# Attention with a sparse feed-forward, head of the kernel: query blocks 0 and 1 taken together key chunk by key chunk, query weights loaded in two pieces, five VectorE tiles in these two blocks

## The chip, the core and the metric

The kernel runs on one core of a Trainium2 chip. The metric is the device time of one launch in microseconds, taken as the median of several runs. The engines are written as in the profile: PE is TensorE (matrix products), DVE is VectorE, ACT is ScalarE, POOL is GpSimd, and SP is the engine that issues most of the DMAs. Each engine works through its own list of instructions in order; semaphores connect the lists.

## What is computed

The input is one sequence of 2048 rows with 448 columns, in bfloat16. The reference is, cut to what matters:

```
xn = layernorm(x)
q  = (xn @ wq) as 16 heads of 28;   k = xn @ wk;   v = xn @ wv     # one key and value head for all
p  = softmax(q k^T / sqrt(28));     h = x + concat_heads(p v) @ wo
hn = layernorm(h);  r = hn @ w_r;   idx = the 8 rows with the largest r
y  = (silu(hn[idx] @ w_gate) * (hn[idx] @ w_up)) @ w_down * sigmoid(r[idx])
out = h + hn,  with y added to the 8 chosen rows
```

Nearly all work is in the attention: 16 heads times 2048 x 2048 exponentials.

## The kernel before

**Blocks and tiles.** The queries are cut into 16 blocks `b`: block `b` holds the 512 query rows of quarter `b // 4` for four heads (group `b % 4`). The keys are cut into 16 tiles `j` of 128 keys; four key tiles make a chunk `c`. One tile `(b, j)` needs the scores of 128 keys against 512 queries in 4 heads. They are made in two halves `p`, each by two matmuls into two banks of PSUM (`qk`).

**Two ways to the exponential.** Most tiles are taken by ACT: each half is one ACTIVATE of 128x1024 with Exp (`act_unit`, L823), into one of six buffers `P`; the two PSUM places alternate, so PE can be two halves ahead. The others are taken by DVE, which makes the exponential out of integer arithmetic (`dve_unit`, L836, and `shift`, L842): four TENSOR_SCALAR of 128x512 out of PSUM banks 4 and 5, then three shifted copies of 128x2048, 7 instructions a tile, in one of three buffers `Y`. Behind an ACT tile stand four matmuls with the values (`act_pv`), behind a DVE tile four for each of its four versions (`dve_pv`). They add up over the 16 key tiles in the bank `acc_bank(b)`, 6 or 7 by turns.

**Who takes what.** The lists `dve_tiles` and `act_tiles` are made at the end of `_main`. Block 0 has no DVE tile, most blocks have four, blocks 5, 9 and 13 have three: 57 DVE tiles and 199 ACT tiles, so 398 ACTIVATEs. Blocks are taken one after the other, key tiles in rising order.

**The head.** `chunk(c)` prepares chunk `c`: layernorm statistics of four x tiles (`bn_stats`, `bn_aggr`), the reciprocal root `rstd`, normalised rows `xn`, transposes on PE, copies `xnT`, the projection to keys with two scaled copies into `K` (one for each `p`), and the projection to values with one scaled copy into `Vs`. `chunk0` is the same for chunk 0, written out by hand in two halves `h`, with the query projection of block 0 in between and 44 matmuls on the identity ahead of it (L350, `ps<-ident`) that compute nothing that is used. Later blocks get their queries from `q_project`. The query weights come in one DMA (`wq_sb`) and are spread into the padded `wq_pad` by two copies on ACT (L405) and two on POOL (L408); every query projection reads all of `wq_pad`. After the head, `last_w` (L726 to L734) makes eight products on DVE that the last block needs.

**After a block** `post_block` copies the accumulated bank to `Ot` (L621), sends the sums through DRAM and divides; after four blocks `out_proj` makes rows of `h` and the second layernorm. The last block and the eight chosen rows have their own code at the end.

**What sets the order.** Nothing in the program's text does it directly. Every operation is recorded with an engine, a cost in nanoseconds, what it reads and writes, and a priority (`G.op`, `G.prio`). `_Graph.plan` then simulates the five engines with these costs and always starts the ready operation with the lowest priority; the lists that come out are emitted as they stand. A cost that is wrong, or a moved priority, thus changes the order on all engines, and an instruction that waits holds up all behind it on its engine. `at(t, ...)` sets the priority of an attention step by its place in the schedule, 16 units a block. Of the recorded functions, L350 is the line of every matmul, L353 that of every transpose, L364 that of every DMA from SP.

Of the kernel before, what the change touches and what calls it, by code (L numbers as in the profile page):

```python
# [6 lines left out]
ACT = mybir.ActivationFunctionType  # L7
# [223 lines left out]
def _main(nc, G, sb, ps, psb, flag, scr, xs, A_x, A_wq, A_wk, A_wv, A_wo, B_w_r, B_w_gate, B_w_up, B_w_down, out,  # L231
# [77 lines left out]
    fin = wq_sb[0:8, 0, :]  # L309
    r12 = sb("r12", [12, 128], F32)  # L310
# [56 lines left out]

    for t in range(4):
# [10 lines left out]
    G.op(PO, lambda e: e.memset(nhalf[:, :], -0.5), 100, writes=["nhalf"])  # L379
    G.op(PO, lambda e: e.iota(pidx[:, :], [[0, 1]], base=0, channel_multiplier=1), 100, writes=["pidx"])  # L380
# [4 lines left out]
    for p in range(2):  # L385
# [10 lines left out]
    G.op(AC, lambda e: e.activation(wk_rep[0:CK, :, :].rearrange("p k (i c) -> p k i c", c=32)[:, :, :, 0:DH],  # L396
                                    wk_sb[0:CK, :, :].unsqueeze(2).broadcast_to([CK, NCH, 4, DH]), ACT.Identity),
         500, reads=["wk_sb"], writes=["wk_rep"])
    G.op(AC, lambda e: e.activation(wv_pad[0:CK, :, 1:1 + DH], wv_sb[0:CK, :, :], ACT.Identity), 200,
         reads=["wv_sb"], writes=["wv_pad"])  # L400
    for ch in range(NCH):
        v = wq_pad[0:CK, ch, :, :].rearrange("p g (i c) -> p (g i) c", c=32)[:, :, 0:DH]
        w = wq_sb[0:CK, ch, :].rearrange("p (h d) -> p h d", d=DH)
        if ch % 2:
            G.op(AC, lambda e, v=v, w=w: e.activation(v, w, ACT.Identity), 480, reads=["wq_sb", "wq_pad"],  # L405
                 writes=[("wq_pad", ch)])
# [69 lines left out]
    def chunk0():  # L476
# [623 lines left out]
```

## Time and profile before

| | |
|---|---|
| median of 3 runs | 415.62 us (415.38 to 415.87) |
| profiled execution | 416.59 us, of which the span of the profile is 414.6 us |
| granted PE clock, mean | 0.967 |
| first and last ACTIVATE of the attention | starts at 15.02 us; the last stretch of 136 starts at 262.50 us and takes 126.17 us |
| ACTIVATEs with Exp of 128x1024 (L823) | 398, 368.5 us busy |
| 128x512 on DVE out of PSUM (L836) | 228, 147.2 us busy |
| shifted copies on DVE (L842) | 171, 114.7 us busy |

The span runs from the first to the last instruction; the profiled execution lies 1.99 us above its own span and 0.97 us above the median of the runs. In the profile, a row of a timeline has the start, the length, the engine, the line, the operation, the tile written and the tile read, and how many instructions of that kind follow one another; in brackets stands how long the engine had been idle ahead of it and who ended the wait. Consecutive instructions of an engine overlap a little, so the pace is the distance from one start to the next, and it is shorter than the length of one.

### The profile page before, as it was taken

The numbers are of one execution on the slowest core, as the hardware profiler recorded it, in microseconds if no ns is written. First come the engines' busy times: TensorE is split into PE (matmuls) and PEld (weight loads), VectorE is DVE, ScalarE is ACT, GpSimd is POOL, SyncE is SP. The second block draws the span as 40 slices with busy tenths as digits, with TensorE's granted clock in tenths as the row PEclk, the third lists the DMA queues.
The fourth block names the chain that finished last, engine by engine and source line by source line (L and its number), as shares of the span: only waits on it lengthen the run. The fifth ranks groups of instructions, "written<-read, shape, count | busy, mean of one in ns | idle before, by whom it ended". The sixth has DMA issues, their size and how long they took to land.

```text
span 414.6 us, 8038 instructions
## 1 busy us (share of the span) xinstructions
PE 349.3 (84%) x3295; PEld 110.5 (27%) x3295; DVE 359.5 (87%) x774; ACT 383.3 (92%) x438; POOL 49.5 (12%) x73
## 2 busy tenths in 40 slices
PE   5978798889888897889898998888888997898845
PEld 5433222222222222222222222222222221222235
DVE  5899979797978899898989999899989999999281
ACT  4779999999999999999999999999999999999640
POOL 7040001010101030100101120101010130312000
PEclk9799999999999999999999999999999999999955
DMA  7794000000000002000010002000000002001000
GB/s 206 173 235 127 2 28 2 21 8 11 20 2 27 4 25 92 27 2 29 0 29 2 7 23 92 26 3 28 2 28 0 27 4 92 28 3 27 3 30 22
DMA packets 17381, 15.73 MB, mean 38 GB/s; under 512 B 5976, under 2 KB 14460, under 8 KB 17340
## 3 DMA queue, kind: packets, MB, share of 16 engines
q1 hardware_dynamic: 17244, 15.16, 13.3%
q8 instruction: 26, 0.43, 0.5%
q14 instruction: 15, 0.12, 0.1%
q0 software_dynamic: 96, 0.02, 0.1%
HBM read 11.70 MB, written 3.47 MB: 37 GB/s over the span
## 4 chain that ended last, share of the span: by engine, by line
ACT 62%; PE 21%; DVE 12%; DMA 2%; issue 1%; SPq 1%; POOL 0%; POOLq 0%; DVEq 0%; ACTq 0%
ACT P L823 62%; PE ps L350 21%; DVE Y L836 2%; DVE Y L842 1%; DVE K L588 1%; DVE Ot L621 1%; DMA wq_sb<-in_A_wq_dram 1%; DVE xnT L581 1%; DMA Lc<-l_scr 1%; SPq L364 1%; DVE bn L547 1%; DMA l_scr<-Ot 1%; DVE xn L565 1%; DVE junk L726 1%; DVE bn L757 1%
## 5 line engine op out<-in xcount | busy, mean ns | idle before, releaser
L823 ACT ACTIVATE P<-ps 128x1024 bf16<-128x1024 f32 x398 | 368.5, 1116 | 5.1 <-PE ps L350 3.9
L350 PE MATMUL ps<-Q,K 64*128 64x512 bf16 x1024 | 182.7, 386 | 45.9 <-ACT P L823 32.3
L836 DVE TENSOR_SCALAR Y<-ps 128x512 int16<-128x512 f32 x228 | 147.2, 682 | 13.9 <-PE ps L350 13.8
L842 DVE TENSOR_SCALAR Y<-Y 128x2048 int16<-128x2048 int16 x171 | 114.7, 705 | 1.6
L350 PEld LDWEIGHTS ps<-Q,K 64*128 64x128 bf16 x1024 | 45.0, 93 | 194.9 <-ACT P L823 157.4
L350 PE MATMUL ps<-P,Vs 128*32 128x512 bf16 x796 | 79.3, 389 | 0.0
L350 PE MATMUL ps<-Y,Vs 128*32 128x512 bf16 x912 | 73.5, 381 | 0.0
L633 POOL TENSOR_TENSOR On<-Ot,Rb 128x512 bf16<-128x512 f32 x15 | 21.4, 1429 | 239.4 <-DMA Rb<-l_scr 239.4
L350 PEld LDWEIGHTS ps<-P,Vs 128*32 128x32 bf16 x796 | 20.4, 92 | 46.7 <-issue 46.6
L350 PEld LDWEIGHTS ps<-Y,Vs 128*32 128x32 bf16 x912 | 23.4, 96 | 17.6 <-issue 7.3
L350 PE MATMUL ps<-xnT,wq_pad 112*128 112x512 bf16 (+1 forms) x68 | 20.1, 393 | 0.6 <-DVE Ot L621 0.6
L350 PE MATMUL ps<-wo_pad,On 128*128 128x448 bf16 (+1 forms) x64 | 17.8, 358 | 2.3 <-DVE Ot L621 1.5
L655 POOL TENSOR_TENSOR st<-st,nhalf 128x1 f32<-128x1 f32 x12 | 10.1, 842 | 64.0 <-DVE st L653 64.0
L463 DVE TENSOR_SCALAR Q<-ps,qone 128x512 bf16<-128x512 f32 x15 | 10.9, 730 | 7.1 <-PE ps L350 7.1
L621 DVE COPY Ot<-ps 128x512 f32<-128x512 f32 x15 | 10.3, 689 | 0.9 <-PE ps L350 0.3
L649 DVE TENSOR_TENSOR hbuf<-ps,x_sb 128x448 f32<-128x448 f32 x12 | 7.5, 622 | 2.5 <-PE ps L350 2.5
L668 DVE SCALAR_TENSOR_TENSOR junk<-hbuf,st,w_rb 128x448 bf16<-128x448 f32 x12 | 8.1, 678 | 0.0
L353 PE MATMUL ps<-ident,xn 128*112 128x128 bf16 x64 | 5.3, 236 | 3.1 <-DVE xn L493 2.7
L651 DVE BATCH_NORM_STATS2 bn<-hbuf 128x6 f32<-128x448 f32 x12 | 7.5, 623 | 0.1
L350 PEld LDWEIGHTS ps<-wo_pad,On 128*128 128x128 bf16 x64 | 4.2, 97 | 11.7 <-issue 6.9
L350 PEld LDWEIGHTS ps<-xnT,wq_pad 112*128 112x128 bf16 x68 | 4.7, 104 | 9.2 <-issue 6.6
L547 DVE BATCH_NORM_STATS2 bn<-x_sb 128x6 f32<-128x448 bf16 x12 | 6.9, 605 | 0.0
(177 smaller groups left out, 169.4 us busy)
## 6 DMA issues: line engine op xcount, KB each, us to landing
Rb<-l_scr SPq DMA_DIRECT2D x15, 256.0 KB
wg_sb<-in_B_w_gate_dram SPq DMA_DIRECT2D x1, 1568.0 KB, 11.9
wu_sb<-in_B_w_up_dram SPq DMA_DIRECT2D x1, 1568.0 KB, 17.9
wd_sb<-in_B_w_down_dram SPq DMA_DIRECT2D x1, 1568.0 KB, 22.1
x_sb<-in_A_x_dram SPq DMA_DIRECT2D x3, 448.0 KB, 5.5
out_dram<-x_sb SPq DMA_DIRECT2D x3, 448.0 KB, 2.8
xn_scr<-xn SPq DMA_DIRECT2D x3, 448.0 KB, 3.8
x_sb<-in_A_x_dram SPq DMA_DIRECT2D x4, 112.0 KB, 2.1
```

Of the source, the lines that this page charges most:

```text
L350: return lambda e: e.matmul(o, lhsT=l, rhs=r, start=start, stop=stop)
L463: G.op(DV, lambda e: e.tensor_scalar(Q[:, b % 4, :], ps[:, bank, :], qone[:, 0:1], None, ALU.add), dvt(512), reads=[pk(bank), "qone"], wri ...
L547: G.op(DV, [lambda e, t=t: e.bn_stats(bn6[:, t, :], x_sb[:, t, 0:D])], 540, reads=[("x", t), ("mv", 4 * c - 1)], writes=[("bn6", t)])
L621: G.op(DV, lambda e: e.tensor_copy(Ot[:, rb, :], ps[:, acc_bank(b), :]), dvt(512), reads=[pk(acc_bank(b))], writes=[("Ot", rb)], prio=u - 30)
L633: G.op(PO, lambda e: e.tensor_tensor(On[:, qb % 2, g, :], Ot[:, rb, :], Rb[:, rb, :], ALU.mult), 1270, reads=[("Ot", rb), ("Rb", rb)], wri ...
L649: G.op(DV, lambda e: e.tensor_tensor(hbuf[:, hr, :], ps[:, bank, 0:D], x_sb[:, t, 0:D], ALU.add), dvt(D), reads=[pk(bank), ("x", t)], writ ...
L651: G.op(DV, lambda e: e.bn_stats(bn6[:, t, :], hbuf[:, hr, :]), dvt(D), reads=[("h", hr)], writes=[("bn6", t)])
L655: G.op(PO, lambda e: e.tensor_tensor(st[:, t, 4:5], st[:, t, 7:8], nhalf[:, 0:1], ALU.pow), 570, reads=[("st7", t), "nhalf"], writes=[("st ...
L668: G.op(DV, lambda e: e.scalar_tensor_tensor(junk[:, :], hbuf[:, hr, :], st[:, t, 4:5], w_rb[:, :], ALU.mult, ALU.mult, accum_out=st[:, t, ...
L823: G.op(AC, lambda e: e.activation(P[:, sl, :, :], ps[:, b0:b0 + 2, :], ACT.Exp, bias=EBIAS, scale=OCT), 905, reads=[pk(b0), pk(b0 + 1)], w ...
L836: G.op(DV, lambda e, k=k: e.tensor_scalar(Y[:, n, 0, p + 2 * k, :].bitcast(I16), ps[:, 4 + k, :], 0.0, 32639.0 - 3 * STEP, ALU.max, ALU.mi ...
L842: G.op(DV, lambda e: e.tensor_scalar(Y[:, n, v, :, :].bitcast(I16), Y[:, n, 0, :, :].bitcast(I16), v * STEP, None, ALU.add), 610, reads=[( ...
```

## The change

The change rearranges the head. All else (the tiles of blocks 2 to 15, the end) keeps its code.

- **Order of the first 32 tiles.** Instead of block 0 and then block 1, the tiles of both go chunk by chunk: four key tiles of block 0, the same four of block 1, then the next chunk. The chunks' own priorities are moved to fit (`8 * c - 3.0`, and events at `4 * c - 20`).
- **DVE tiles.** Blocks 0 and 1 have five instead of four: key tiles 5 and 9 in both blocks and 13 in block 0. That makes 58 DVE tiles and 198 ACT tiles, 396 ACTIVATEs.
- **Query weights.** They are loaded in two DMAs: the 112 columns of group 0 between the keys' and the values' weights, and the other 336 columns after them. `wq_pad` is filled group by group, group 0 on ACT, behind the second `rstd`, the three others on POOL. A query projection waits for its own group alone. `wk_rep` on ACT comes after the first `rstd`, and `wv_pad` moves from ACT to POOL.
- **Chunk 0.** All statistics come first, then the four normalised tiles; the second pair of statistics waits for the first. Order of the projections is Q, K, Q, K by halves. The scaled copies of the second half of K and the copy of the first half of Q move from ACT to DVE. 56 identity matmuls stand ahead instead of 44, and 16 more (`warm(4)` four times) between the transposes.
- **Chunk 1** gets `rstd` from POOL (`pow`) like chunks 2 and 3, no longer from two ACT instructions. Chunks 1 to 3 use two PSUM banks (4 and 5) by turns, no longer three, and their key projection is recorded in two pieces.
- **Query projections** of blocks 1, 2 and 3 get places of their own: that of block 1 in bank 4, that of block 2 in bank 4 at 24.0, that of block 3 at 34.5. `last_w` has the priority of 72 instead of 40.

The list that the planner makes of this can be read from the built program: on PE, 58 identity matmuls stand ahead of the first transpose and 2, 7, 1 and 4 behind the four groups of transposes; the first score matmuls of a DVE tile stand behind those of the 30th ACTIVATE (before: behind the 21st), and on DVE all DVE tiles stand behind the value copy of chunk 3, as before.

```diff
     for t in range(4):
-        dma(x_sb[:, t, 0:D], x_v[:, t, :], [("x", t)], lat=2700.0 + 250 * t)
-    dma(wk_sb[0:CK, :, :], A_wk.rearrange("(k p) n -> p k n", p=CK), ["wk_sb"], lat=4000.0)
-    dma(wv_sb[0:CK, :, :], A_wv.rearrange("(k p) n -> p k n", p=CK), ["wv_sb"], lat=4000.0)
-    dma(wq_sb[0:CK, :, :], A_wq.rearrange("(k p) n -> p k n", p=CK), ["wq_sb"], lat=5500.0)
+        dma(x_sb[:, t, 0:D], x_v[:, t, :], [("x", t)], lat=2700.0 + 350 * t)
+    dma(wk_sb[0:CK, :, :], A_wk.rearrange("(k p) n -> p k n", p=CK), ["wk_sb"], lat=4500.0)
+    dma(wq_sb[0:CK, :, 0:CK], wq_v[:, :, 0:CK], [("wq", 0)], lat=5000.0)
+    dma(wv_sb[0:CK, :, :], A_wv.rearrange("(k p) n -> p k n", p=CK), ["wv_sb"], lat=5500.0)
+    dma(wq_sb[0:CK, :, CK:D], wq_v[:, :, CK:D], [("wq", 1)], lat=6500.0)
...
+    for _ in range(56):
+        G.op(PE, mm(ps[:, 7, 0:128], ident[:, :], ident[:, :], True, True), 85, reads=["ident"], writes=[pk(7)])
...
-    for ch in range(NCH):
-        v = wq_pad[0:CK, ch, :, :].rearrange("p g (i c) -> p (g i) c", c=32)[:, :, 0:DH]
...
+    def pad_wq(g, eng):
+        v = wq_pad[0:CK, :, g, :].rearrange("p k (i c) -> p k i c", c=32)[:, :, :, 0:DH]
+        w = wq_sb[0:CK, :, g * CK:g * CK + CK].rearrange("p k (i d) -> p k i d", d=DH)
...
-        for _ in range(44):
-            G.op(PE, mm(ps[:, 7, 0:128], ident[:, :], ident[:, :], True, True), 107, reads=["ident"], writes=[pk(7)],
-                 prio=-900)
...
+        q_half(0)
+        k_half(0, AC)
+        q_half(1)
+        k_half(1, DV)
         v_project(0, 5)
-        G.prio = 9
-        q_project(1, MISC)
+        G.prio = -0.5
+        q_project(1, 4)
...
-        G.prio = 4 * c - 7
+        G.prio = 8 * c - 3.0
...
-            return (7, 4, 5)[hb[0] % 3]
+            return 4 + hb[0] % 2
...
-    groups[0] = 0
+    FD, FN, FT, FS = (5, 9, 13), 5, 18.5, 2.8
...
+    first = [(b, j) for c in range(4) for b in range(2) for j in range(4 * c, 4 * c + 4)]
+    early = [(b, j) for j in FD for b in range(2)][:FN]
+    for n, (b, j) in enumerate(early):
+        dve_tiles.append((b, j, FT + FS * n))
+    left = [p for p in first if p not in early]
+    for n, (b, j) in enumerate(left):
+        act_tiles.append((b, j, 32.0 * n / len(left)))
+    for b in range(2, NB):
...
-    events = [(4.0 * c - 9.0, lambda c=c: chunk(c)) for c in range(4)]
+    events = [(4.0 * c - 20.0, lambda c=c: chunk(c)) for c in range(4)]
...
-        if b + 2 < NB:
+        if 1 < b < NB - 2:
             at(16 * b + 6.5, q_project, b + 2, misc_bank(b))
...
-    at(16 * 2 + 8.0, last_w)
+    at(24.0, q_project, 2, 4)
+    at(16 * 2 + 2.5, q_project, 3, misc_bank(2))
+    at(16 * 4 + 8.0, last_w)
```

More of the change, by code (lines that the diff above doesn't have):

```diff
@@ L474, in v_project, with warm @@
                                            ALU.mult), 620, reads=[pk(bank), "vcc"], writes=[("V", c)])
+    def warm(n, prio):
+        for _ in range(n):
+            G.op(PE, mm(ps[:, 7, 0:128], ident[:, :], ident[:, :], True, True), 80, reads=["ident"], writes=[pk(7)],
+                 prio=prio)
     def chunk0():
         G.prio = -500
[L478 to L480 removed]
@@ new lines, in q_half @@
+            bank = 6 + h
+            G.op(PE, [mm(ps[:, bank, 0:256], wq_pad[0:CK, ch, 0, :], xnT[0:CK, 0, ch, c], ch == 0, ch == NCH - 1)
+                      for ch in range(NCH)], 4 * 115, reads=[("wqp", 0), ("xnT", 0, 2 * h), ("xnT", 0, 2 * h + 1)],
+                 writes=[pk(bank)])
+            G.op(DV, lambda e: e.tensor_scalar(Q[:, 0, c], ps[:, bank, 0:256], qone[:, 0:1], None, ALU.add), 400,
+                 reads=[pk(bank), "qone"], writes=[(("Q", "Qh")[h], 0)])
+        q_half(0)
```

136 lines of the change are left out of this document (65 added, 71 removed).

## The prediction

> **What bounds the kernel now.** I read the page first: shares of the engines, the chain that ended last, the costliest groups.
>
> ```profile
> span 414.6 us, 8038 instructions
> ...
> PE 349.3 (84%) x3295; PEld 110.5 (27%) x3295; DVE 359.5 (87%) x774; ACT 383.3 (92%) x438; POOL 49.5 (12%) x73
> ...
> ACT 62%; PE 21%; DVE 12%; DMA 2%; issue 1%; SPq 1%; POOL 0%; POOLq 0%; DVEq 0%; ACTq 0%
> ...
> L823 ACT ACTIVATE P<-ps 128x1024 bf16<-128x1024 f32 x398 | 368.5, 1116 | 5.1 <-PE ps L350 3.9
> L836 DVE TENSOR_SCALAR Y<-ps 128x512 int16<-128x512 f32 x228 | 147.2, 682 | 13.9 <-PE ps L350 13.8
> L842 DVE TENSOR_SCALAR Y<-Y 128x2048 int16<-128x2048 int16 x171 | 114.7, 705 | 1.6
> ```
>
> ACT leads, DVE is near. An average hides the stages, so next come the windows view of the exponentials alone (L823), and that of all engines over the attention.
>
> ```profile
> 15.00:39.74 24.74, 21.11 (x22) 0.99 0.84 199
> 39.74:388.70 348.96, 347.35 (x376) 1.00 0.07 22
> ```
>
> ```profile
> 40.00:388.00 348.00, 303.30 (x2749) 82.54 (x2745) 313.59 (x617) 346.43 (x376) 34.39 (x29) 1.00 0.07 22
> ```
>
> From 39.74 us on ACT is full: 376 exponentials in 347.35 us, a **pace of 0.924 us** each, with 1.6 us of gaps. The first 22 took 24.74 us where the pace gives 20.3: **4.4 us are lost in the head**, and the first one starts only at 15.02. DVE is idle 348.0 - 313.6 = **34.4 us** of the body. So the body is bound by the number of ACT exponentials; the head is bound by what feeds them. ACT's timeline and the chain that ended last, over the head, tell by what:
>
> ```profile
> 6.38 0.20 ACT L489 ACTIVATE rstd<-var 128x2 f32<-128x2 f32 x1
> 7.74 1.04 ACT L405 ACTIVATE wq_pad<-wq_sb 112x448 bf16<-112x448 bf16 x2 [1.06 <-DMA wq_sb<-in_A_wq_dram]
> 8.78 1.06 ACT L501 ACTIVATE xnT<-ps 112x512 bf16<-112x512 bf16 x2
> 14.11 1.02 ACT L525 ACTIVATE K<-ps,kb,ksc 128x256 bf16<-128x256 f32 x2 [1.18 <-PE ps L350]
> 15.02 1.94 ACT L823 ACTIVATE P<-ps 128x1024 bf16<-128x1024 f32 x2
> 20.51 2.87 ACT L823 ACTIVATE P<-ps 128x1024 bf16<-128x1024 f32 x3 [0.53 <-PE ps L350]
> 25.14 4.93 ACT L823 ACTIVATE P<-ps 128x1024 bf16<-128x1024 f32 x5 [1.76 <-PE ps L350]
> 39.75 222.25 ACT L823 ACTIVATE P<-ps 128x1024 bf16<-128x1024 f32 x240 [0.34 <-PE ps L350]
> ```
>
> ```profile
> 3.60 4.06 DMA wq_sb<-in_A_wq_dram
> ...
> 10.66 3.43 PE ps L350 x16
> ...
> 23.94 1.43 DVE K L588 x2
> ...
> 30.30 1.44 DVE K L588 x2
> ...
> 35.98 1.46 DVE K L588 x2
> ```
>
> The chain runs: the one DMA of the query weights (landed at 7.66), the pads on ACT, which hold up the second `rstd` and the first `xnT`, then 16 projection matmuls in 3.43 us, then the first exponential. After that the chain goes through DVE: the keys of chunks 1, 2 and 3 are there at 25.4, 31.7 and 37.4, and block 0 alone eats a chunk in 8 exponentials, 7.4 us. ACT waits for DVE's chunks, through PE.
>
> **Part 1, the start of the exponentials.** The DMA and the pads leave the chain: group 0 has a quarter of the bytes, and its one pad stands behind both `rstd`. What is late next is PE's list, where 58 identity matmuls come first.
>
> ```profile
> 1.80 4.28 PE L350 MATMUL ps<-ident 128*128 128x128 bf16 x44 [1.80 <-POOL ident L377]
> 20.08 0.61 PE L350 MATMUL ps<-Q,K 64*128 64x512 bf16 x4
> ```
>
> ```profile
> 5.00:6.00 1.00, 1.00 (x16) 0.90 (x14) 0.41 (x3) 0.62 (x2) 1.00 (x12) 1.00 0.66 143
> 7.00:8.00 1.00, 0.74 (x8) 0.58 (x8) 0.32 (x2) 0.26 (x1) 0.29 (x1) 1.00 1.12 308
> 12.00:13.00 1.00, 1.00 (x6) 0.70 (x5) 0.18 (x1) 0.93 (x3) 0.00 (x0) 0.50 0.34 88
> 5.30:8.70 3.40, 1.51 (x21) 1.18 (x19) 0.81 (x3) 2.22 (x8) 1.69 (x11) 1.00 1.01 301
> 387.60:391.00 3.40, 2.81 (x19) 0.94 (x17) 0.76 (x2) 1.19 (x3) 0.00 (x0) 1.00 0.00 0
> 391.00:394.40 3.40, 1.82 (x6) 0.68 (x6) 2.38 (x10) 1.90 (x6) 0.00 (x0) 1.00 0.03 5
> ```
>
> The 44 end at 6.08; 14 more at the pace of the last ones (16 in 1 us, 0.0625) take 0.9, at the mean pace (4.28 / 44 = 0.097) 1.4: they end between 6.95 and 7.45; I take 6.95, since the last ones are the nearest. The first `rstd` was done at 6.58 behind two pads that now stand elsewhere, so `xn` is no later than that. Eight transposes took 0.74, so the first tile's are through at 7.35 and the second's, behind 2 more identity matmuls, at 7.8. ACT: `xnT` 0.53 (1.06 / 2), pad 0.52 (1.04 / 2), `xnT` 0.53: 7.4 to 9.0. Meanwhile transposes three and four, with 8 identity matmuls between, end near 8.9, and DVE's two copies near 9.5:
>
> ```profile
> 2.83 1.15 DVE L482 BATCH_NORM_STATS2 bn<-x_sb 128x6 f32<-128x448 bf16 x2 [1.01 <-DMA x_sb<-in_A_x_dram]
> 10.27 0.85 DVE L504 COPY xnT<-ps 112x512 bf16<-112x512 bf16 x2 [0.47 <-PE ps L353]
> 13.26 0.48 DVE L520 TENSOR_SCALAR Q<-ps,qone 128x256 bf16<-128x256 f32 x1 [1.08 <-PE ps L350]
> 60.08 1.28 DVE L836 TENSOR_SCALAR Y<-ps 128x512 int16<-128x512 f32 x2
> 61.27 1.28 DVE L842 TENSOR_SCALAR Y<-Y 128x2048 int16<-128x2048 int16 x2
> 62.48 0.69 DVE L836 TENSOR_SCALAR Y<-ps 128x512 int16<-128x512 f32 x1
> ```
>
> The 16 projections ran at a granted clock of 0.50 (12 to 13 us). At full clock they take half of 3.43: from 9.05 to about 10.8. Behind them on DVE stand one copy of Q (0.48), one `bn_stats` (1.15 / 2) and the other copy of Q: the second half of Q is there near 11.0. The last two K copies no longer stand ahead of the exponential on ACT. From score matmuls to the exponential are 0.43 (20.08 to 20.51): first exponential at **11.6**; at half clock at 9.05 + 3.43 + 0.5 + 0.43 = 13.4. Which clock? It had fallen after a stretch of 3.4 us in which PE was busy 1.51 (5.30 to 8.70), and fell again after one with 1.82 (391.0 to 394.4), while one with 2.81 (387.6 to 391.0) left it at 1.00. After the change PE has work all through 5.3 to 8.9. So it should hold: 11.6, **3.4 us earlier**.
>
> [...]
>
> **Part 2, gaps in the head.** Chunks are now needed at exponentials 17, 29 and 41 (8 tiles, then 6, then 6 on ACT), that is at 11.6 + 16 x 0.924 = 26.4, then 37.5 and 48.6. DVE had the keys at 25.4, 31.7 and 37.4; its copies of `xnT`, from which its chain goes on, end near 9.5 instead of at 11.1, and it gets two K copies of 0.51 and a Q copy of 0.48 more to do, and ahead of the keys of chunk 3 three products of `last_w` that stood behind them, 0.60 each if they are like Y. So the keys come at about 25.3, 31.6 and 39.1, and no chunk is late, the first by a margin of 1.1. What remains is order on PE: some score matmuls stand behind transposes of the next chunk. I keep 0.5 of the 4.4 us: **-3.9**. Bounds: 0 and 2.3 (the two largest gaps, 0.53 and 1.76, come back).
>
> **Part 3, one tile less on ACT:** 2 exponentials, **-1.85**. The seven instructions more on DVE take 0.60 each (60.08, 61.27, 62.48: two and two in 2.40), 4.2 us, beside 34.4 us of idle time.
>
> **Part 4, DVE loses its lead.**
>
> ```profile
> 38.53 1.29 DVE L836 TENSOR_SCALAR Y<-ps 128x512 int16<-128x512 f32 x2
> ```
>
> ```profile
> PEld ps L350 <- DVE Y L836: 15.6, 37, 1.2
> DVE Y L836 <- PE ps L350: 13.8, 25, 1.1
> ```
>
> Its tiles start where they did, at 38.5, but there ACT stood at exponential 22, and now at 30. Until the list has caught up, PE, which keeps order, holds score matmuls for ACT behind matmuls on DVE's results. By the order of the built program the worst place is exponential 65, behind the values of the third shifted copy of tile (2, 1). For that copy DVE has 44 instructions of 0.60 (26.4), two copies to `Ot` and two of Q at about 0.66 (2.6), small ones (0.4), and waits for PE of 13.8 / 25 = 0.55 at some six score pairs (3.3 to 3.6): done at 38.5 + 32.9 = 71.4, and three groups of value matmuls later the scores can run: 72.5. ACT would be there at 11.6 + 0.5 + 64 x 0.924 = 71.2. That and a smaller one before give **+1.7**. After it a block has 28 x 0.60 + 1.7 = 18.5 us on DVE against 24 x 0.924 = 22.2 on ACT, and DVE gains again. Bounds: 0 (exponentials start later and DVE is in time) and 4.3 (0.06 more for each of the 44, as the groups' means of 147.2 / 228 = 0.646 and 114.7 / 171 = 0.671 have it).
>
> **Edits costed at nothing.** POOL's pads, `wv_pad` and `rstd` of chunk 1 lie beside 88% idle on POOL; a late `rstd` would delay chunk 1, with its margin of 1.1. The added DMA moves the x loads on SP by one issue (0.43 to 0.49):
>
> ```profile
> 4.00:5.00 1.00, 1.00 (x13) 1.00 (x11) 0.00 (x0) 1.00 0.78 58
> ```
>
> Here the narrow `wk` and `wv` rows kept the DMA engines busy 0.78 at 58 GB/s; the later x tiles are first read behind the first copy of Q, near 10. If they land 1 us late, that stands ahead of the second copy of Q and costs 1 us. [...]
>
> **Sum:** -3.4 - 3.9 - 1.85 + 1.7 = -7.45. Span 414.6 to 407.15; the execution is 1.99 longer than its span (416.59), so 409.1; the median of the runs is 0.97 below the profiled one, so **408.2 us**.
>
> **Rivals.**
> - *The start comes at half clock* (0.13). PE's busy time is modelled and the bound lies somewhere between 1.82 and 2.81 of 3.4; then 13.4 instead of 11.6: **410.0**. For it: a single stretch decides. The same would follow if the clock rose later than in the row from 5 to 6 us, since the identity matmuls then end later and the projections run slow. Against: the three runs lie within 0.5 us. [...]
> - *DVE's catching up costs 4.3* (0.15): **410.8**, and 412.5 if block 3 pays as well. For it: PE's weight loads already wait 15.6 us for Y. Against: ACT hardly noticed.
> - *DVE sets the end* (0.06), the slower side. If DVE from 38.5 on had no idle time, its one tile more would add 7 x 0.60 = 4.2: **419.8**. It decides once the 34.4 us of idle time are used up by waits; nothing in the trace takes that much.
> - *The gains are swallowed by PE's order in the head* (0.04): Part 2 and Part 4 at their worst and the half clock together, 415.6 - 1.6 - 2.1 - 1.85 + 4.3 = **414.4**, or no change if one more place of 1.2 comes.
>
> **Chances and range.** Forecast 0.62, with its own range of 406.4 to 409.6. A run of this kernel tells 0.2% from no change. Faster 0.91, same 0.03, slower 0.06. The range takes in the first two rivals above and, below, Part 4 at 0 with a start at 11.1: **405.5 to 412.5**.
>
> **What would show it.** Right: a first exponential between 11.2 and 12; granted clock 1.00 from 9 to 12; the 23rd exponential near 32.4 instead of 39.75; ACT's largest gap near 70 us, behind PE; 396 ACTIVATEs. Wrong: `xnT` waiting for identity matmuls; DVE's first statistics of chunk 1 waiting for a DMA; gaps of ACT after 100 us, behind Y; an ACT pace above 0.93.

## The result, and the profile after

The changed kernel takes **412.36 us** (median of 6 runs, 411.80 to 414.31) where the kernel before took 415.75 beside it (6 runs, 415.07 to 416.82): a ratio of 0.9928, 95% interval 0.9906 to 0.9949. That is 3.4 us faster. The forecast was 408.2, with an own range of 406.4 to 409.6; the sign was right, the gain was under half of the one forecast, and the wider range of 405.5 to 412.5 just holds the measured time. A second measurement (`e7_after_again`, below) gave 412.64 us, ratio 0.9944 (0.9920 to 0.9968).

The profiled execution took 414.31 us, the longest of the six; its span is 412.2. The page, with the shares of the engines, the chain that ended last, and the costliest groups:

```profile
span 412.2 us, 8124 instructions
...
PE 352.7 (86%) x3335; PEld 110.9 (27%) x3335; DVE 366.0 (89%) x785; ACT 381.1 (92%) x429; POOL 51.3 (12%) x76
...
ACT 54%; PE 27%; DVE 16%; issue 1%; DMA 1%; POOL 0%; SPq 0%; POOLq 0%; DVEq 0%
...
L845 ACT ACTIVATE P<-ps 128x1024 bf16<-128x1024 f32 x396 | 368.1, 1089 | 6.3 <-PE ps L351 4.3
...
L858 DVE TENSOR_SCALAR Y<-ps 128x512 int16<-128x512 f32 x232 | 149.5, 680 | 13.2 <-PE ps L351 12.7
L864 DVE TENSOR_SCALAR Y<-Y 128x2048 int16<-128x2048 int16 x174 | 119.0, 715 | 1.5
```

The lines have moved by some twenty: L845 is now the exponential, L858 the DVE copy out of PSUM, L864 the shifted copy, L351 the matmuls. Two exponentials less, as announced, yet ACT's share of the last chain went from 62 to 54% and PE's from 21 to 27%: ACT waits for PE more often (ahead of exponentials 8 times, 4.3 us in all, where it was 6 times and 3.9 us). ACT's timeline tells where:

```profile
10.86 1.02 ACT L527 ACTIVATE K<-ps,kb,ksc 128x256 bf16<-128x256 f32 x2 [1.14 <-PE ps L351]
12.40 53.81 ACT L845 ACTIVATE P<-ps 128x1024 bf16<-128x1024 f32 x58 [0.52 <-PE ps L351]
66.48 1.94 ACT L845 ACTIVATE P<-ps 128x1024 bf16<-128x1024 f32 x2 [0.27 <-PE ps L351]
69.25 1.94 ACT L845 ACTIVATE P<-ps 128x1024 bf16<-128x1024 f32 x2 [0.83 <-PE ps L351]
72.23 56.40 ACT L845 ACTIVATE P<-ps 128x1024 bf16<-128x1024 f32 x61 [1.04 <-PE ps L351]
```

The head is as forecast: one run of 58 exponentials without a gap, 53.81 / 58 = 0.928 us each; the five gaps of before between 20 and 40 us are gone. New are the gaps at 66 to 72 us. The windows view of the exponentials alone, for the same 22 us in the kernel after and, below it, before (columns: length, busy time with the number of instructions, granted clock, DMA share, GB/s):

```profile
55.00:77.00 22.00, 19.74 (x22) 1.00 0.06 16
```

```profile
55.00:77.00 22.00, 22.00 (x25) 1.00 0.05 14
```

To add up such losses over a whole execution I take the starts of the exponentials from the trace and subtract 0.9167 us from each step; 24 steps in 22.0 us is what the undisturbed blocks of before need. What is left over in a stretch is its loss. Steps are counted from the first exponential. "Last" is the end of the last exponential. All numbers are us, each row is one profiled execution; steps 25-48 lose nothing in any of them (0.4 in `e1`). From the fourth row on they are the experiments that follow.

| kernel | exps | first | steps 1-24 | 49-72 | 73-216 | from 217 | last |
|---|---|---|---|---|---|---|---|
| before | 398 | 15.02 | 4.55 | 0.01 | 1.08 | 3.20 | 388.67 |
| after, first profile | 396 | 12.40 | 0.12 | 2.82 | 4.14 | 3.69 | 386.22 |
| after, second profile (`e7_after_again`) | 396 | 11.63 | 0.12 | 2.83 | 2.81 | 3.89 | 384.32 |
| `e1_four_tiles` | 398 | 11.09 | 0.31 | 1.61 | 3.02 | 3.17 | 384.52 |
| `e2_not_merged` | 398 | 12.46 | 6.76 | 0.41 | 1.58 | 3.21 | 389.23 |
| `e3_fewer_identity` | 396 | 11.06 | 3.98 | 2.82 | 2.81 | 2.60 | 386.32 |
| `e4_block2_three` | 398 | 11.89 | 0.13 | 2.14 | 1.17 | 3.77 | 383.98 |
| `e5_short_shifts` | 396 | 11.52 | 0.12 | 2.82 | 3.29 | 3.78 | 384.57 |
| `e8_block2_lc` | 398 | 12.55 | 2.56 | 2.03 | 2.43 | 2.99 | 387.43 |
| `e9_tile_9` | 396 | 11.70 | 0.13 | 2.28 | 1.26 | 7.03 | 385.44 |
| `e11_short_told` | 396 | 11.63 | 0.13 | 2.27 | 1.53 | 2.99 | 381.60 |
| `e13_eight_p` | 396 | 11.99 | 0.13 | 1.20 | 2.12 | 4.18 | 382.68 |
| `e16_eight_p_lc` | 396 | 11.41 | 0.12 | 1.31 | 3.41 | 3.51 | 382.81 |
| `e17_eight_p_three` | 398 | 11.38 | 0.13 | 0.65 | 1.12 | 3.31 | 381.47 |
| `e15_before_eight_p` | 398 | 12.92 | 4.46 | 0.00 | 2.78 | 2.52 | 387.47 |
| `e18_before_warm` | 398 | 12.99 | 4.46 | 0.00 | 1.70 | 2.44 | 386.38 |

The first profile of after has 1.3 us of its 4.14 from a half clock at 157.7 to 161.1 us, which the second does not have; so the second is the one to compare with. It is, however, the fastest of its twelve runs.

### The profile page after: what moved, and what is told of

Read it like the earlier page. It is cut to its first block, busy times and chain, and to the rows that moved or that the text cites. A ratio compares the mean times of both kernels' runs of the same rounds, so it can differ in the third digit from the quotient of the medians.

```text
span 412.2 us, 8124 instructions
## 1 busy us (share of the span) xinstructions
PE 352.7 (86%) x3335; PEld 110.9 (27%) x3335; DVE 366.0 (89%) x785; ACT 381.1 (92%) x429; POOL 51.3 (12%) x76
## 3 DMA queue, kind: packets, MB, share of 16 engines
HBM read 11.70 MB, written 3.47 MB: 37 GB/s over the span
## 4 chain that ended last, share of the span: by engine, by line
ACT 54%; PE 27%; DVE 16%; issue 1%; DMA 1%; POOL 0%; SPq 0%; POOLq 0%; DVEq 0%
ACT P L845 53%; PE ps L351 27%; DVE Y L858 7%; DVE Y L864 6%; DVE Ot L636 1%; DMA Lc<-l_scr 1%; DVE bn L772 1%; ACT K L527 0%; DVE idx L972 0%; ACT xn L789 0%; POOL out_dram L1038 0%; DVE On L630 0%; SPq L365 0%; DVE wq_sb L1037 0%; DVE ra L778 0%
## 5 line engine op out<-in xcount | busy, mean ns | idle before, releaser
L845 ACT ACTIVATE P<-ps 128x1024 bf16<-128x1024 f32 x396 | 368.1, 1089 | 6.3 <-PE ps L351 4.3
L351 PE MATMUL ps<-Q,K 64*128 64x512 bf16 x1024 | 183.0, 386 | 42.1 <-ACT P L845 29.5
L858 DVE TENSOR_SCALAR Y<-ps 128x512 int16<-128x512 f32 x232 | 149.5, 680 | 13.2 <-PE ps L351 12.7
L864 DVE TENSOR_SCALAR Y<-Y 128x2048 int16<-128x2048 int16 x174 | 119.0, 715 | 1.5
L351 PEld LDWEIGHTS ps<-Q,K 64*128 64x128 bf16 x1024 | 43.9, 93 | 188.2 <-ACT P L845 146.8
L351 PE MATMUL ps<-P,Vs 128*32 128x512 bf16 x792 | 78.4, 390 | 0.0
L351 PE MATMUL ps<-Y,Vs 128*32 128x512 bf16 x928 | 77.7, 382 | 0.1
L648 POOL TENSOR_TENSOR On<-Ot,Rb 128x512 bf16<-128x512 f32 x15 | 22.4, 1496 | 235.9 <-DMA Rb<-l_scr 235.9
L351 PEld LDWEIGHTS ps<-P,Vs 128*32 128x32 bf16 x792 | 20.1, 93 | 46.1 <-issue 45.5
L351 PEld LDWEIGHTS ps<-Y,Vs 128*32 128x32 bf16 x928 | 23.6, 95 | 24.5 <-issue 12.4
L351 PE MATMUL ps<-xnT,wq_pad 112*128 112x512 bf16 (+1 forms) x68 | 19.3, 377 | 1.4 <-DVE Ot L636 1.2
L351 PE MATMUL ps<-wo_pad,On 128*128 128x448 bf16 (+1 forms) x64 | 17.8, 358 | 2.6 <-DVE Ot L636 1.8
L351 PE MATMUL ps<-ident 128*128 128x128 bf16 x72 | 7.6, 287 | 1.8 <-POOL ident L380 1.8
L351 PEld LDWEIGHTS ps<-ident 128*128 128x128 bf16 x72 | 6.9, 134 | 1.8 <-POOL ident L380 1.8
L351 PEld LDWEIGHTS ps<-wo_pad,On 128*128 128x128 bf16 x64 | 4.2, 97 | 11.8 <-issue 7.9
L351 PEld LDWEIGHTS ps<-xnT,wq_pad 112*128 112x128 bf16 x68 | 4.4, 98 | 10.2 <-issue 4.2
```

Of the source, the lines that this page charges most:

```text
L351: return lambda e: e.matmul(o, lhsT=l, rhs=r, start=start, stop=stop)
L648: G.op(PO, lambda e: e.tensor_tensor(On[:, qb % 2, g, :], Ot[:, rb, :], Rb[:, rb, :], ALU.mult), 1270, reads=[("Ot", rb), ("Rb", rb)], wri ...
L845: G.op(AC, lambda e: e.activation(P[:, sl, :, :], ps[:, b0:b0 + 2, :], ACT.Exp, bias=EBIAS, scale=OCT), 905, reads=[pk(b0), pk(b0 + 1)], w ...
L858: G.op(DV, lambda e, k=k: e.tensor_scalar(Y[:, n, 0, p + 2 * k, :].bitcast(I16), ps[:, 4 + k, :], 0.0, 32639.0 - 3 * STEP, ALU.max, ALU.mi ...
L864: G.op(DV, lambda e: e.tensor_scalar(Y[:, n, v, :, :].bitcast(I16), Y[:, n, 0, :, :].bitcast(I16), v * STEP, None, ALU.add), 610, reads=[( ...
```

## The experiments

**First round: is it VectorE's lag, or the clock?** Theory A: DVE has lost its lead, and PE, which keeps order, holds ACT's scores up behind it. Theory B: the loss comes from the late rise of PE's clock at the start (7.51 us) and a dip later (0.50 from 157.7 to 161.1 us), both seen in the first profile. Four kernels take the change apart. Before, measured beside them: 415.42 us.

`e1_four_tiles`: no fifth DVE tile.

```diff
-    FD, FN, FT, FS = (5, 9, 13), 5, 18.5, 2.8
+    FD, FN, FT, FS = (5, 9, 13), 4, 18.5, 2.8
```

> The changed kernel with four instead of five DVE tiles in blocks 0 and 1 (key tiles 5 and 9 of both); ACT has 398 exponentials again, 1.85 us more than the changed kernel (412.4). Theory A, DVE lost its lead and holds ACT's score matmuls up through PE's order: the gaps at 57 to 75 us (2.8 us beyond the pace) mostly go and the body after 100 us loses 1 to 2 us less, so 410 to 412.5. Theory B, the shortfall is the PE clock (a late rise at the start, a dip in the body) and DVE's load does not matter: 414.2, with the gaps at 57 to 75 us as they were.

Measured: 413.07 us, ratio 0.9932 (0.9911 to 0.9954). The fifth tile brings at most part of its 1.85: what two exponentials more cost here, the stretch 49-72 gives back in good part (2.8 to 1.6). That decides nothing between A and B, but gaps remain with one DVE tile less.

`e2_not_merged`: all parts of the change but the merging (and its DVE tiles).

```diff
-    first = [(b, j) for c in range(4) for b in range(2) for j in range(4 * c, 4 * c + 4)]
-    early = [(b, j) for j in FD for b in range(2)][:FN]
+    first = []
+    early = []
...
-    for b in range(2, NB):
+    groups[0] = 0
+    for b in range(NB):
```

> The changed kernel with blocks 0 and 1 one after the other and their tiles shared out as before (none on DVE in block 0, four in block 1); 398 exponentials; all else of the change stays. If taking the two blocks together is what feeds ACT in the head: first exponential still near 12.4, but 3 to 4.4 us of gaps from there to 40 us, as before, and few gaps at 57 to 75 us: 414 to 416. If the start alone made the gain (rival): the gaps merely moved, and 412 to 413.5.

Measured: 416.53 us, ratio 1.0021 (0.9995 to 1.0048). Nothing of the gain is left, although the first exponential is at 12.46. ACT's timeline shows who took it back:

```profile
12.46 7.52 ACT L846 ACTIVATE P<-ps 128x1024 bf16<-128x1024 f32 x8 [0.52 <-PE ps L351]
23.88 1.94 ACT L846 ACTIVATE P<-ps 128x1024 bf16<-128x1024 f32 x2 [3.90 <-PE ps L351]
26.31 2.17 ACT L846 ACTIVATE P<-ps 128x1024 bf16<-128x1024 f32 x2 [0.49 <-PE ps L351]
```

Block 0 alone has eaten chunk 0 after 8 exponentials, at 20.0, and chunk 1 comes when it comes: 3.90 us of waiting. Here the earlier start is worth nothing, since nothing is there to do until the next chunk. The two gains of the head are not two independent terms: without the merging, the first is lost. (The 6.76 us of this profile are not owed to the missing merging alone: the granted clock was 0.50 from 24.7 to 31.5 us, behind the longest gap. And `e18` below shows that a head in which the chunks come earlier too keeps an earlier start.)

`e3_fewer_identity`: 44 identity matmuls ahead instead of 56, none between the transposes.

```diff
-    for _ in range(56):
+    for _ in range(44):
...
-            warm(4, -500)
+            warm(0, -500)
```

> The changed kernel with 44 identity matmuls ahead, as before, and none between the transposes. If these matmuls only stand in the way of the transposes: the first transpose starts near 6.5 instead of 7.7 and the first exponential near 11.3 instead of 12.4, and the time is 411 to 412. If they keep the clock up (rival): the granted clock is 0.50 during the 16 projections, the first exponential is at 12.8 to 13.5 and the time 412.5 to 414.

Measured: 412.26 us, ratio 0.9913 (0.9882 to 0.9945), no difference from after. Its profiled execution did start early, at 11.06, and lost it again at 21 us, in a way that no theory had. DVE's timeline, then the windows of all engines (columns: PE, PEld, DVE, ACT, POOL busy, granted clock, DMA share, GB/s):

```profile
20.87 0.62 DVE L451 TENSOR_REDUCE sw<-w_rb 128x1 f32<-128x448 bf16 x1 [1.95 <-DMA w_rb<-in_B_w_r_dram]
```

```profile
18.30:21.60 3.30, 1.68 (x18) 0.81 (x16) 1.35 (x4) 3.03 (x4) 0.00 (x0) 1.00 0.97 271
21.70:28.40 6.70, 6.26 (x42) 1.55 (x42) 5.92 (x17) 3.60 (x4) 2.42 (x3) 0.50 1.04 235
```

A sum over the router's weights, needed at the end of the kernel, stands in the middle of DVE's head and waited 1.95 us for its DMA; behind it stood the last copy of `xnT` for chunk 1, PE ran dry (1.68 of 3.30 busy), and the clock went to 0.50 for 6.8 us. That is one execution, the slowest of its four runs (411.98 to 414.05); the median does not show it.

`e4_block2_three`: three DVE tiles in block 2 instead of four.

```diff
+    groups[2] = 3
     where = {0: (), 1: (9,), 2: (5, 11), 3: (3, 7, 11), 4: (1, 5, 9, 13), 5: (1, 4, 7, 10, 13)}
```

> The changed kernel with three instead of four DVE tiles in block 2 (five stay in blocks 0 and 1); 398 exponentials. Theory A (lead): DVE catches up one tile, 4.2 us, sooner, the gaps at 57 to 66 us stay (0.9 us), those at 66 to 75 us go, and the body loses 1 to 2 us less: 410.5 to 412.5. Theory B (clock): 414.2.

Measured: 411.92 us, ratio 0.9902 (0.9868 to 0.9936). Two exponentials more cost 1.83 us, and the kernel is no slower: the loss in steps 73-216 fell from 2.8 to 1.17, about what before has (1.08). So one DVE tile in block 2 is worth nothing, and the losses after step 72 hang on it. That is what A said of this stretch; whether DVE is late on the chip or the planner writes another order is left to `e5` and `e11`. In steps 49-72 2.14 of 2.83 remain, and that is not what A said.

**Second round: take VectorE's work away.** If A also holds for the gaps at 57 to 75 us, they must shrink when DVE has less to do there. Before, measured beside these: 415.55 us.

`e5_short_shifts`: the shifted copies of eight DVE tiles leave out three quarters of their columns; the planner is told nothing of it, so all lists keep their order.

```diff
-        G.op(DV, lambda e: e.tensor_scalar(Y[:, n, v, :, :].bitcast(I16), Y[:, n, 0, :, :].bitcast(I16),
+        w = 1 if 3 <= m < 11 else 4
+        G.op(DV, lambda e: e.tensor_scalar(Y[:, n, v, 0:w, :].bitcast(I16), Y[:, n, 0, 0:w, :].bitcast(I16),
```

> The changed kernel with the shifted copies of eight VectorE tiles (numbers 3 to 10) cut to a quarter of their columns, the order of all instructions unchanged; what is left out is three quarters of these copies, about 24 x 0.45 = 10.8 us of VectorE's time between 52 and 130 us. Theory A (VectorE falls behind in the merged blocks and through PE's order holds ScalarE's scores up): the gaps of 2.8 us at 57 to 75 us shrink to 1 or less and the excess of the steps from 72 to 216 from 1.7 to about 1: 408.0 to 409.5. Theory B (the order on PE or the clock makes these gaps by itself): they stay, 411.5 to 412.5.

Measured: 412.35 us, ratio 0.9932 (0.9906 to 0.9958): nothing gained, in steps 73-216 either (3.29 us lost, 2.81 in `e7`), of which the short copies cover the part up to some 130 us. **Theory A falls for these gaps.** The 24 copies did get short (the groups view, shapes apart), and ACT's gaps came at the same exponentials with the same lengths to 0.01 us:

```profile
L865 DVE TENSOR_SCALAR Y<-Y 128x512 int16<-128x512 int16 x24 | 6.1, 285 | 0.1
```

```profile
66.58 0.68 DVE L636 COPY Ot<-ps 128x512 f32<-128x512 f32 x1
67.91 0.40 PE L351 MATMUL ps<-P,Vs 128*32 128x512 bf16 x4
68.36 1.94 ACT L845 ACTIVATE P<-ps 128x1024 bf16<-128x1024 f32 x2 [0.83 <-PE ps L351]
71.34 1.94 ACT L845 ACTIVATE P<-ps 128x1024 bf16<-128x1024 f32 x2 [1.04 <-PE ps L351]
```

`e7_after_again`: the changed kernel, unaltered.

> The changed kernel as it is, for a second profile on the same chip as the others: 411.8 to 413. If the time of the clock's rise sets the start, a run that rises before 5.5 us has its first exponential at 11.0 to 11.3, and one that rises after 7 us near 12.4; the gaps at 57 to 75 us are the same 2.8 us either way.

Measured: 412.64 us, ratio 0.9944 (0.9920 to 0.9968); the profiled execution took 411.84. The first exponential came between the two expected places, at 11.63, and the gaps are the same 2.8 us. The whole timeline around the largest gaps, cut to the instructions that matter:

```profile
65.82 0.62 PE L351 MATMUL ps<-Y,Vs 128*32 128x512 bf16 x8
...
67.10 0.68 DVE L636 COPY Ot<-ps 128x512 f32<-128x512 f32 x1
...
67.70 0.10 PEld L351 LDWEIGHTS ps<-Q,K 64*128 64x128 bf16 x2 [0.37 <-ACT P L845]
...
68.02 0.40 PE L351 MATMUL ps<-P,Vs 128*32 128x512 bf16 x4
...
68.47 1.94 ACT L845 ACTIVATE P<-ps 128x1024 bf16<-128x1024 f32 x2 [0.83 <-PE ps L351]
...
71.01 0.39 PE L351 MATMUL ps<-P,Vs 128*32 128x512 bf16 x4
...
71.45 1.94 ACT L845 ACTIVATE P<-ps 128x1024 bf16<-128x1024 f32 x2 [1.04 <-PE ps L351]
```

Read it backwards from 68.47, with the code beside it. This is the 61st exponential. Its scores had been made at 66.8, so it does not wait for scores. It writes buffer 60 % 6 = 0 of the six `P`, which the 55th wrote for key tile (2, 0); the value matmuls of that tile, at 68.02 to 68.42, must have read it. The built program says the same: its 61st and 63rd exponential wait for the value matmuls of block 2 that read P buffers 0 and 2. Of the 2.83 us, these two steps hold 0.93 and 1.14; of the rest, 0.49 before the 51st is a wait for a P buffer too, which value matmuls of block 0 have to read, and 0.39 before the 59th is a wait for scores. The value matmuls of block 2 are that late because they open the accumulator of block 2, `acc_bank(2)` = bank 6, which is that of block 0 as well. Block 0 ends only with the last version of its DVE tile (0, 13), at 65.82 to 66.44, and DVE copies the bank to `Ot` at 67.10. In the kernel before, block 0 was long done by then (the copies to `Ot` start at 50.00 for block 0 and 71.86 for block 1); merged, blocks 0 and 1 hold both banks until the end (62.90 and 67.10).

**Theory C**: ACT fills its six buffers, three key tiles, and then waits for the first value matmuls of block 2; and these stand where the written order has them, behind score matmuls that themselves wait for ACT (67.70). This explains `e5`: the copy to `Ot` came 0.4 us sooner there, counted from the first exponential, and the value matmuls stayed where the list has them. The accumulator thus acts through the written order: the planner puts these matmuls behind the copy in its own simulation.

**Theory D**: PE simply has too much work there. The windows view has it full for 4 us, though not for the next two:

```profile
62.00:64.00 2.00, 2.00 (x24) 0.50 (x22) 1.97 (x4) 2.00 (x3) 0.00 (x0) 1.00 0.00 0
64.00:66.00 2.00, 2.00 (x16) 0.62 (x14) 2.00 (x5) 1.73 (x3) 0.00 (x0) 1.00 0.01 4
66.00:68.00 2.00, 1.52 (x14) 0.39 (x10) 2.00 (x4) 1.65 (x2) 0.00 (x0) 1.00 0.04 4
```

`e8_block2_lc`: as `e4`, and the planner is told longer times for the two DMAs of a block's sums.

```diff
-            dma(scr[b, 0], Ot[0:128:32, rb, :], [("scr0", b)], reads=[("Ot", rb)])
-        dma(Lc[:, rb, :], scr[b, 0].rearrange("i (r k) -> (i r) k", k=16), [("Lc", rb)], reads=[("scr0", b)])
+            dma(scr[b, 0], Ot[0:128:32, rb, :], [("scr0", b)], reads=[("Ot", rb)], lat=3000.0)
+        dma(Lc[:, rb, :], scr[b, 0].rearrange("i (r k) -> (i r) k", k=16), [("Lc", rb)], reads=[("scr0", b)], lat=3500.0)
```

> Block 2 with three VectorE tiles, and the planner told that the two DMAs of a block's sums take 3.0 and 3.5 us instead of 2.0 each, so that VectorE meets the minimum, maximum and reciprocal of the sums later. Theory A: VectorE's waits for these DMAs of up to 1.9 us, behind which Y and then the scores stand, go away and the single long steps with them: 410.5 to 411.3. Rival: they are hidden nearly always, 411.9 as with three tiles in block 2 alone.

Measured: 412.17 us, ratio 0.9919 (0.9887 to 0.9950), as `e4` within the interval, and not the 410.5 to 411.3 of A. (Its profiled execution, 415.25, is the slowest of its eight and had 7 us of half clock in the head, which its steps 1-24 show.)

`e9_tile_9`: a DVE tile moved from block 2 to block 9.

```diff
+    groups[2], groups[9] = 3, 4
```

> One VectorE tile moved from block 2 to block 9: 396 exponentials as in the changed kernel, but VectorE gets 4.2 us back in the catch-up and pays them at 240 us. Theory A (only the lead is short in the catch-up): the gaps at 56 to 80 us as with three tiles in block 2 (2.1), the excess to 216 us near 1, 410 to 411. Rival (VectorE has no idle time to spend in any block): a gap of over 1 us near block 9 and 411.5 to 412.5.

Measured: 412.78 us, ratio 0.9921 (0.9892 to 0.9951), 0.3 above the rival's range and far from that of A. Steps 73-216 are as cheap as in `e4` (1.26), and from 217 on 7.03 us are lost where after has 3.89; ACT waits 1.04 us at the ninth exponential of block 10, which follows the full block:

```profile
254.37 56.82 ACT L846 ACTIVATE P<-ps 128x1024 bf16<-128x1024 f32 x61 [1.04 <-PE ps L351]
```

One half-clock stretch of 3.4 us at 340 us is in these 7.03 too. Neither of the two blocks tried, 2 and 9, takes the fourth tile for nothing.

**Third round: the buffers.** Before, beside these: 415.54 us.

`e13_eight_p`: eight buffers `P` instead of six. (The room comes from `idi`, a helper of the start that now lies in a buffer used later.)

```diff
-    NPB = 6
+    NPB = 8
...
-    idi = sb("idi", [128, 128], I32)
...
     hbuf = sb("hbuf", [128, 4, D], F32)
+    idi = hbuf[:, 0, 0:128].bitcast(I32)
```

> The changed kernel with eight P buffers instead of six, so that ScalarE can be four key tiles ahead of the value matmuls and not three. Theory C: ScalarE's gaps before exponentials 61 and 63 (0.9 and 1.1 us), which end with value matmuls of block 2, go, the gaps at 57 to 75 us fall from 2.8 to 1 or less: 410.0 to 411.0. Theory D (PE is full there) or A (VectorE late): the gaps come elsewhere, 412 to 412.5.

Measured: **410.11 us**, ratio 0.9865 (0.9840 to 0.9891). That is faster than both kernels (the kernel after had ratios of 0.9928 and 0.9944). The exponentials in the same 22 us as above, and ACT's timeline:

```profile
55.00:77.00 22.00, 21.30 (x24) 1.00 0.06 16
```

```profile
11.99 59.41 ACT L845 ACTIVATE P<-ps 128x1024 bf16<-128x1024 f32 x64 [0.52 <-PE ps L351]
72.00 19.52 ACT L845 ACTIVATE P<-ps 128x1024 bf16<-128x1024 f32 x21 [0.61 <-PE ps L351]
```

ACT is busy 21.30 of 22.00 us where it was 19.74, and the stretch 49-72 loses 1.20 instead of 2.83, a little more than the 1 that C allowed. D said that the gaps come elsewhere; most do not. The edit also moves PE's list, since the planner knows of the eight buffers. But block 0 is copied no sooner, counted from the first exponential, and the value matmuls of key tile (2, 0) come even later than in `e7` (68.02), while ACT runs on:

```profile
67.54 0.69 DVE L636 COPY Ot<-ps 128x512 f32<-128x512 f32 x1
...
68.86 0.40 PE L351 MATMUL ps<-P,Vs 128*32 128x512 bf16 x4
```

The largest gap left, 0.61 at 72.00, stands before the 65th exponential; in the built program that one waits for a P buffer again.

`e15_before_eight_p`: the same edit in the kernel before.

> The kernel before with eight P buffers. Theory C: its blocks end one after the other, its accumulator comes free in time and no exponential waits for a P buffer, so nothing is gained: 415.0 to 416.0. If eight buffers help every block (more slack on PE), it gains 1 to 3 us as well and the gain of eight buffers in the changed kernel is not owed to the merging.

Measured: 415.69 us, ratio 1.0011 (0.9990 to 1.0032). Eight buffers are worth nothing there, and the lists of the built program are those of before, entry by entry. So of these two kernels the six bind only in the one that merges two blocks: **C stands**, for the gaps before the 61st and the 63rd exponential.

`e11_short_told`: the short copies of `e5`, and the planner knows that they are short.

```diff
-                                           v * STEP, None, ALU.add), 610,
+                                           v * STEP, None, ALU.add), 610 if w > 1 else 270,
```

> The same shortened shifted copies as before (eight VectorE tiles, three quarters of each copy left out), and now the planner is told that such a copy takes 0.27 us instead of 0.61, so that PE's written order may use VectorE's time. The shortening alone left the gaps of ScalarE at 57 to 75 us as they were, since the order was already written. Theory C (a block's accumulator and six P buffers: block 2's first value matmuls must wait until block 0's last ones are through and copied, ScalarE fills six P buffers meanwhile and then waits): block 0 ends some 2 us earlier, the gaps fall from 2.8 to about 1.5 and the time to 410.5 to 411.5. Theory D (PE simply has too much work there): 412 to 412.5.

Measured: 410.11 us, ratio 0.9869 (0.9843 to 0.9895), 2.2 us less than `e5` with the same instructions in another order. The time is a little better than C had it, but not for C's reason: the gain lies mostly in the stretches behind. 73-216 fell from 3.29 to 1.53, 49-72 only from 2.82 to 2.27, where C had about 1.5; the copy of block 0 came 1.2 us sooner than in `e7` (65.89 for 67.10), not 2. So DVE's time does count, but through the order that the planner writes with it; shorter copies in the old order gained nothing.

`e16_eight_p_lc`: eight buffers and the longer DMA times of `e8`.

> The changed kernel with eight P buffers and with the planner told that the two DMAs of a block's sums take 3.0 and 3.5 us. If both help, 409.5 to 410.5; if the waits for these DMAs are hidden, as eight P buffers alone.

Measured: 410.54 us, ratio 0.9877 (0.9852 to 0.9902), as eight buffers alone within the interval. The profiles speak against the longer times, both here and in `e8`: steps 73-216 lose 1.3 us more with them (3.41 for 2.12, and 2.43 for 1.17).

**Fourth round: what was still open.** Before, beside these: 415.81 us.

`e17_eight_p_three`: eight buffers and three DVE tiles in block 2.

> The changed kernel with eight P buffers and with three VectorE tiles in block 2: both remedies. If the lost time between exponentials 72 and 216 (2.1 us with eight P buffers) comes from block 2's fourth VectorE tile, it falls to about 1.1, while two exponentials more cost 1.83: 410.0 to 411.0, the two remedies do not add up. If they do: 409.0 to 409.7.

Measured: 410.80 us, ratio 0.9879 (0.9844 to 0.9914), the first of the two cases: the losses fall to 0.65 and 1.12, the lowest of all, and two exponentials more take that back. It does not beat `e13`.

`e18_before_warm`: the kernel before, with 20 identity matmuls in PE's idle time between the transposes.

```diff
+                for _ in range(20 if t == 1 else 0):
+                    G.op(PE, mm(ps[:, 7, 0:128], ident[:, :], ident[:, :], True, True), 2, reads=["ident", ("xn", t)], writes=[pk(7)])
```

> The kernel before with 20 identity matmuls more, between the first two pairs of transposes, where PE was idle for 1.75 us; nothing else is changed and no other order moves. If the half clock in the head is what most of the executions of before pay, the granted clock stays 1.00 from 5 to 14 us, the first exponential comes at 12.9 to 13.3 instead of 15.0, and the time is 413.5 to 414.5: then some 1 to 2 us of the forecast's 3.4 at the start belong to the clock alone. If it is an accident of the one profiled execution: 415.2 to 415.8.

Measured: 414.49 us, ratio 0.9969 (0.9948 to 0.9989). The windows from 9 to 12 us, before and then with the 20 matmuls:

```profile
9.00:12.00 3.00, 2.45 (x16) 2.02 (x17) 2.53 (x6) 1.30 (x3) 1.44 (x10) 0.50 0.66 208
```

```profile
9.00:12.00 3.00, 2.44 (x24) 2.03 (x24) 2.78 (x7) 2.09 (x5) 1.45 (x10) 1.00 0.73 237
```

PE is as busy in both, but at full clock it does 24 matmuls instead of 16, and the first exponential comes at 12.99 instead of 15.02. So 2.0 of the 3.4 us at the start are the clock's alone, in this pair of executions; in the medians the 20 matmuls are worth 1.3 (0.5 to 2.2 by the interval). The whole head moves with the clock: the 9th exponential, the first that needs chunk 1, starts at 23.02 instead of 25.14.

## Why the prediction was right in sign and too high in size

Its sum, beside what the two profiles (before 416.59; the second profile of after, 411.84, the fastest of its runs) show:

| step | forecast | measured |
|---|---|---|
| start of the exponentials | -3.4 | -3.4 (15.02 to 11.63; first profile 12.40, -2.6) |
| gaps in the head | -3.9 | -4.4 |
| one tile less on ACT | -1.85 | -1.83 |
| catching up, steps 49-72 | +1.7 | +2.8 |
| steps 73-216 | 0 | +1.7 |
| steps from 217, and the end | 0 | +0.7 - 0.4 |
| sum | -7.45 | -4.7 |
| from the profiled pair to the medians | -0.97 | none; the median of after lies 0.5 to 0.8 above its second profile |

- **Right:** the full clock from 9 to 12 us (1.00 in the first profile), the 23rd exponential (32.4 forecast; 32.72 and 31.95), 396 ACTIVATEs, the head without gaps, the largest gap of ACT near 70 us behind PE. The first exponential (11.6 forecast, a band of 11.2 to 12) came at 12.40 and 11.63; the near hit is luck in part, since the place of the clock's rise, taken from one execution, moves it (4.56 us in `e1`, with the first exponential at 11.09, and 7.51 in the first profile of after, with 12.40).
- **Wrong, the step that after the catch-up a block has 18.5 us on DVE against 22.2 on ACT, "and DVE gains again".** The sums of the windows view over 13 blocks, 78 to 372 us after and 80 to 372 before:

```profile
sum 294.00, PE 257.37 PEld 68.65 DVE 275.53 ACT 290.63 POOL 31.48; mean PE 19.80 PEld 5.28 DVE 21.19 ACT 22.36 POOL 2.42
```

```profile
sum 292.00, PE 255.57 PEld 69.42 DVE 267.93 ACT 290.50 POOL 28.98; mean PE 19.66 PEld 5.34 DVE 20.61 ACT 22.35 POOL 2.23
```

  DVE has 21.2 us of work in a stretch of 22.6 (294 / 13), about one block, not 18.5 in 22.2. The row for it stood in the profile before: DVE 20.6. The 18.5 counted the tiles, `Ot` and Q, and left out the rows of the output that four blocks later go through DVE:

```profile
L664 DVE TENSOR_TENSOR hbuf<-ps,x_sb 128x448 f32<-128x448 f32 x12 | 7.4, 616 | 0.6 <-PE ps L351 0.6
L666 DVE BATCH_NORM_STATS2 bn<-hbuf 128x6 f32<-128x448 f32 x12 | 7.4, 620 | 0.1
L677 DVE TENSOR_SCALAR x_sb<-hbuf,st 128x448 bf16<-128x448 f32 x12 | 6.1, 508 | 0.0
L680 DVE TENSOR_SCALAR xn<-hbuf,st 128x448 bf16<-128x448 f32 x12 | 6.1, 506 | 0.0
L683 DVE SCALAR_TENSOR_TENSOR junk<-hbuf,st,w_rb 128x448 bf16<-128x448 f32 x12 | 8.1, 677 | 0.0
```

  35.1 us over 12 blocks, 2.9 each. With 1.4 us of slack, waits included, DVE can hardly regain its lead, and the loss goes on until step 216: +1.7. The runs show that this loss goes with the order that the planner writes from DVE's costs: `e4` and `e11` take it away, `e5`, shorter copies in the old order, does not. That the small slack is what makes this order is argued, not shown. The planner's own simulation of the two programs, with its 0.905 us an exponential, already has both losses: 0.13 us before and 3.51 after in steps 49-72, 2.34 and 3.82 in steps 73-216. The +0.7 behind step 216 is not explained; the other kernels without a dip there lose 2.4 to 4.2.
- **Wrong mechanism, the step that a shifted copy is done at 71.4 "and three groups of value matmuls later the scores can run".** The place was near, the cause another: not scores behind a late DVE copy (`e5`), but, for 2.07 of the 2.83 us, exponentials behind value matmuls of block 2, whose accumulator block 0 still held (`e13`, `e15`). The forecast looked at who makes an instruction's input and not at who must free its output. Measured 2.8 instead of 1.7.
- **Wrong, the step "the median of the runs is 0.97 below the profiled one".** It carries the profiled pair's gain over to the median whole. But the start term was read from an execution that paid for the half clock; 2.0 us of it are the clock. Not every execution of before pays it: `e15`'s profile, before but for the buffers, began its exponentials at 12.92, and holding the clock brings 1.3 in the median. Having taken the half clock away in the first term, the sum took it away once more in the last. How many executions of before pay it is not known, but the runs give a hint: of the 77 runs of before in the four rounds, 27 have a mean granted clock of 0.968 or less, as the profiled one (0.967), and take 416.5 us in the median; the other 50 take 415.1. The mean does not tell where in the execution the clock fell. These 77 runs lie between 413.25 and 418.20, not "within 0.5 us" like the three that the forecast had.
- **The rivals.** That DVE's catching up costs 4.3, "and 412.5 if block 3 pays as well", came out in number (2.8 + 1.7 = 4.5), but by the causes above; that is luck. The start at half clock did not come; the start varies with the length of the 58 identity matmuls (4.71 us in `e1`, 6.26 in `e8`) instead, which the same rival mentions. The lower bound of the range does not follow from the two terms named for it: 408.2 - 1.7 - 0.5 is 406.0, not 405.5.

## What to carry to other kernels

When two units of work are merged, list what each holds and when it lets go: banks and buffers that were freed one after the other are then held together, and an engine that runs ahead fills its ring and stops, as ACT did here ahead of the 61st and the 63rd exponential (0.93 and 1.14 us in `e7`). A lead of one engine over another is budgeted with the measured busy time of a whole period, not with the instructions that one thinks of. A list that a planner writes carries its waits with it: here they stand in the planner's own simulation, and shortening the work without writing the list anew gained nothing. And a gain read from one execution contains what that execution had by chance; it must not be taken off again on the way to the median.

## What the runs showed of the hardware that was not expected

The same 58 identity matmuls, started at 1.79 us every time, took from 4.71 us (`e1`) to 6.26 (`e8`); shown are `e1` and the first profile of after, with 6.12:

```profile
1.79 4.71 PE L351 MATMUL ps<-ident 128*128 128x128 bf16 x58 [1.79 <-POOL ident L380]
```

```profile
1.79 6.12 PE L351 MATMUL ps<-ident 128*128 128x128 bf16 x58 [1.79 <-POOL ident L380]
```

The first exponential moved with them, 11.09 and 12.40. The clock record of the trace has the rise at 4.56 us in the one and at 7.51 in the other. So the rise moves by 3 us between these two executions.

And the clock fell once in the middle of the attention, for a single stretch. Below are the 3.4 us ahead of it and the stretch itself:

```profile
154.28:157.70 3.42, 1.97 (x18) 0.60 (x18) 3.07 (x10) 3.42 (x5) 0.03 (x1) 1.00 0.23 76
157.70:161.10 3.40, 3.40 (x18) 0.52 (x18) 3.40 (x6) 2.67 (x3) 0.00 (x0) 0.50 0.59 196
```

Only the first profile of after, `e15` and `e9` show such a dip, at 158, 161 and 341 us; it costs some 1.3 us (4.14 - 2.81). As far as the records show, PE had less work just ahead of all three: busy 1.97, 2.03 and 2.08 us of 3.4, where 3.4 us of the body of after have 2.98 in the mean (257.37 / 294.00 x 3.4). That alone does not decide it: the first 3.4 us after the rise in `e15` (7.83 to 11.24) have 1.75, and the clock stayed at 1.00. So the bound that the first rival put between 1.82 and 2.81 us of 3.4 is not shown by the runs. What sets the dip off is open.
